# Chunked SSM scan plus SiLU MLP on one core: how unit 2 gets its decays, which queues carry the early loads, and the order of unit 0's scan

## The chip, the cores and the metric

The kernel runs on one core of one Trainium2 chip. The metric is device time in microseconds (us), median of three runs; lower is better. The core's engines each work through their own list of instructions in order: TensorE (PE, matrix products), VectorE (DVE), ScalarE (ACT), GpSimd (POOL), and SyncE (SP), which here only issues transfers. ACT and POOL can issue transfers too, from their own lists. An engine that waits for a semaphore holds everything behind it in its list.

## The reference

Two parts are computed, one feeding the other. First a state-space scan over x (batch 4, 8 heads, 768 steps, 32 values a step), with a decay a per step and vectors B and C of 16:

```python
log_a = np.log(np.clip(a, 1e-06, 1.0))
# per chunk: cum = cumsum(log_a); L = exp(cum_i - cum_j), causal
y = (C B^T * L) x + (C state) * exp(cum)
state = exp(sum(log_a)) * state + sum_j B_j x_j exp(cum_last - cum_j)
```

Then, with the heads of one step side by side (3072 rows of 256 values), a two-layer network: `h = x @ w_in` (256 to 2048), `g = h * sigmoid(h)`, `out = g @ w_out` (2048 to 256). The weights come in as float64.

## The kernel before, in words

**Units.** The 3072 rows are cut into 12 units of 256 steps, three per batch. A unit has four chunks of 64 steps (Q = 64). Units 0 to 2 are batch 0. The network works on pairs of units; P = 0 is the pair of units 0 and 1, which has its own start-up form, and P = 1 to 5 are the rest.

**One unit's scan.** The decays, bounded to [1e-6, 1], are needed in two layouts. `PZ[u]` (tiles pz, pz1, pz3: 4 chunks of 65, a row per head and state index) feeds the prefix products `PFX` (f_P, line 336). `ab[u]` (64 steps of a chunk broadcast over partitions, first column zero) feeds the decay matrices `E` (scan_E, line 344). f_T or f_TP make transposed B and C (bh, ct); f_T2 makes ce (line 391); f_C makes cw (line 395); f_B makes BT (line 368); f_G and f_D0 are the products C B and B x on PE (lines 425, 411); f_S and f_SM carry the state (lines 443, 445, 452); f_M multiplies by E (line 431); f_Y sums the unit's output on PE (465, 474), and f_X copies it to `XF[u]` (484). In the schedule texts the letters P, T, C, 1, 2, B, D, S, s, M, Y stand for these, so "2:PTC1" is a stretch of unit 2; "a" issues the next unit's ab, "L" all loads of a unit.

**Where the decays come from.** For units 0 and 1 raw a is loaded already broadcast (load_a, tile pa01) and bounded on chip (f_P0, line 332); their ab is made by PE from the tile ach with a selection matrix (f_Ab, line 351; f_A bounds ach, line 266). For units 2 to 11, all of a is loaded in chunk layout (tile acl, line 258), bounded (f_A2, line 272), and written to two arrays in DRAM, a_in and a_zero, by two transfers that ACT issues (273, 274). load_pa (106) and load_ab (113) read them back broadcast. The tiles ab and pz have one buffer each, so unit 3's ab may be loaded only when unit 2's E is done.

**Weights.** Sixteen blocks of 512 KB (load_w, 186), w0 to w7 of the first layer and w8 to w15 of the second, pass through six raw buffers. float64 becomes float32 by two ACT steps (w_size, lines 192 and 195: wu, wv), three DVE steps and an add on POOL (w_bits, 200 to 208: w32). Later each block is split into high, low and rest parts (w_h, w_l, w_d: steps h, l, d of the texts).

**The network.** For P = 0, f_s1(u, j) multiplies unit u with block j and applies SiLU (514, 517); f_s2 is the second layer (527; the steps m0 to m7). For the other pairs it is s1_d, s1_h, s1_g, s2 and s2_d (542, 550, 558, 560, 584, 585, 598), driven by step(s), with scans of later units in between. PSUM gives two buffers to f_s1's output, which f_TP's transposes and the dummy products of busy(n) share; TP's buffer is held until cw has read it.

**What sets the order.** The order on every engine is written out by hand (manual schedule): the calls at the top issue the first loads, a list of calls runs unit 0 and unit 1's scan, and the texts in `steps` and the loop behind it say what follows each f_s1 and f_s2: "b5" is w_bits(5), "s6" w_size(6), "r11" the load of block 11. Nearly all loads stand in SP's list. The program shares eight semaphores among the transfers that SP and ACT issue. An issue that takes a semaphore in turn waits until that semaphore's earlier transfer has landed, whichever of the two queues issued it. A tile with no free buffer makes the issue wait for the tile's last reader as well. Transfers issued by POOL have semaphores of their own.

Of the kernel before, what the change touches and what calls it, by code (L numbers as in the profile page):

```python
# [8 lines left out]
FP32 = mybir.dt.float32  # L9
# [24 lines left out]
def kernel(  # L34
# [69 lines left out]
    def load_pa(u, q):  # L104
        PZ[u] = pz if u != 3 else block("pz3")[:, 0:4 * Q + 4].rearrange("p (c t) -> p c t", c=4)
        q.dma_start(out=PZ[u].rearrange("p c t -> p (c t)"),
                    in_=a_in[:, 4 * u:4 * u + 4].rearrange("h (o c) t -> h o (c t)", o=1).to_broadcast([H, N, 4 * Q + 4]))

    def load_ab(u, q):
        ab[u] = loads.tile([128, 2, H, Q], FP32, name="ab")  # L110
        for t in range(4):
            k, c = divmod(t, 2)
            q.dma_start(out=ab[u][64 * c:64 * c + 64, k], in_=a_zero[4 * u + t:4 * u + t + 1].to_broadcast([64, H, Q]))
# [115 lines left out]
    a_in = dram.tile([H, batch * S // Q, Q + 1], FP32, name="a_in")  # L229
    a_zero = dram.tile([batch * S // Q, H, Q], FP32, name="a_zero")  # L230
    NC0 = S // Q
    A0, A1 = 96, 96 + NC0
    ach = block("ach").rearrange("p (h t) -> p h t", t=Q)
    nc.sync.dma_start(out=ach[A0:A1], in_=bass.AP(tensor=a.tensor, offset=a.offset, ap=[[Q, NC0], [S, H], [1, Q]]))
    pa01 = block("pa01")
# [4 lines left out]
    def load_a(u, q):  # L240
        q.dma_start(out=pa01[:, UT * u:UT * u + UT],
                    in_=bass.AP(tensor=a.tensor, offset=a.offset + UT * u, ap=[[S, H], [0, N], [1, UT]]))

    load_a(0, nc.scalar)
    load_t(0, 1, nc.sync)
    load_n(0, 0, nc.scalar)
    load_x(0, nc.sync)
    load_w(0, nc.sync)
    load_a(1, nc.sync)
    for n in range(1, 3):  # L250
        load_w(n, nc.sync)
    load_n(1, 0, nc.sync)
    load_n(1, 1, nc.sync)
    load_x(1, nc.sync)

    acl = block("acl").rearrange("p (h t) -> p h t", t=Q)
    for b in range(batch):
        nc.sync.dma_start(out=acl[NC0 * b:NC0 * b + NC0],
                          in_=bass.AP(tensor=a.tensor, offset=a.offset + b * H * S, ap=[[Q, NC0], [S, H], [1, Q]]))

    for n in range(3, RAW):
        load_w(n, nc.sync)
    load_n(2, 1, nc.sync)

    def f_A():
        nc.vector.tensor_scalar(out=ach[A0:A1], in0=ach[A0:A1], scalar1=1.0, scalar2=1e-6, op0=ALU.min, op1=ALU.max)
        nc.vector.memset(ach[A0:A1, :, 0:1], 0.0)

    def f_A2():

        r = slice(0, NC0 * batch)
        nc.vector.tensor_scalar(out=acl[r], in0=acl[r], scalar1=1.0, scalar2=1e-6, op0=ALU.min, op1=ALU.max)
        nc.scalar.dma_start(out=a_in[:, :, 1:].rearrange("h c t -> c h t"), in_=acl[r])
        nc.scalar.dma_start(out=a_zero[:, :, 1:], in_=acl[r, :, 1:])
# [5 lines left out]
    def f_A0():  # L280
        for t in (a_in[:, :, 0:1].rearrange("h c t -> c h t"), a_zero[:, :, 0:1]):
            nc.gpsimd.dma_start(out=t, in_=misc[:NC0 * batch, 0:H].rearrange("p (h t) -> p h t", t=1))
# [38 lines left out]
    nc.scalar.activation(diag, diag1.to_broadcast([128, H, Q]), AF.Copy)  # L321
# [330 lines left out]
    for e in range(2):  # L652
        f_T2(0, e)
# [243 lines left out]
```

## Time and profile before

| | |
|---|---|
| median of three runs | 341.19 us (339.53 to 342.89) |
| profiled execution | 342.16 us, of which the span 340.4 us |
| granted TensorE clock, mean | 0.988 of full |
| busy in the span | PE 322.7 us, DVE 251.7, ACT 219.0, POOL 71.4 |
| moved by the DMA engines | 30.85 MB, mean 91 GB/s |

The span runs from the first to the last instruction of the program; the rest of the time lies around it. The page's busy share of PE is an average over the whole span: where the profile is cut into windows, the start-up with P = 0 (about the first 63 us) looks unlike the rest. In the timeline, a bracket after a group of instructions gives the idle time of the engine just before it and what ended it. A name ending in q is an engine's sequencer, where transfers are issued. A float32 product shows as two records a call.

### The profile page before, as it was taken

The numbers are of one execution on the slowest core, as the hardware profiler recorded it, in microseconds if no ns is written. First come the engines' busy times: TensorE is split into PE (matmuls) and PEld (weight loads), VectorE is DVE, ScalarE is ACT, GpSimd is POOL, SyncE is SP. The second block draws the span as 40 slices with busy tenths as digits, with TensorE's granted clock in tenths as the row PEclk, the third lists the DMA queues.
The fourth block names the chain that finished last, engine by engine and source line by source line (L and its number), as shares of the span: only waits on it lengthen the run. The fifth ranks groups of instructions, "written<-read, shape, count | busy, mean of one in ns | idle before, by whom it ended". The sixth has DMA issues, their size and how long they took to land.

```text
span 340.4 us, 7774 instructions
## 1 busy us (share of the span) xinstructions
PE 322.7 (95%) x3136; PEld 256.8 (75%) x3136; DVE 251.7 (74%) x416; ACT 219.0 (64%) x418; POOL 71.4 (21%) x71
## 2 busy tenths in 40 slices
PE   7877994999999999999999999999999999999993
PEld 3556783888877778777778778778778778888882
DVE  6885784998568797998766897865996863484453
ACT  3645685376359889757775856676666756666651
POOL 4433240537101113033101331202231202000000
PEclk9997999899999999999999999999999999999999
DMA  6986869854665484244340153430153000012003
GB/s 144 192 217 167 251 143 325 199 97 77 122 135 88 92 159 79 58 112 79 64 95 0 43 113 66 91 67 0 48 109 64 2 2 0 0 24 40 0 0 62
DMA packets 97423, 30.85 MB, mean 91 GB/s; under 512 B 82284, under 2 KB 88684, under 8 KB 97388
## 3 DMA queue, kind: packets, MB, share of 16 engines
q1 hardware_dynamic: 87812, 25.32, 32.3%
q0 software_dynamic: 2368, 4.20, 7.0%
q10 hardware_dynamic: 7208, 0.85, 1.7%
q8 instruction: 24, 0.39, 0.5%
q14 instruction: 11, 0.09, 0.1%
HBM read 22.82 MB, written 3.34 MB: 77 GB/s over the span
## 4 chain that ended last, share of the span: by engine, by line
PE 83%; DMA 5%; SPq 5%; DVE 3%; ACT 1%; issue 1%; DVEq 0%; ACTq 0%
PE hp L550 23%; PE b L598 11%; PE hp L542 11%; PE oa L584 10%; PE oa L585 10%; PE oa L527 8%; PE hp L514 3%; SPq L123 2%; PE gy L474 2%; PE gy L465 2%; DMA tbc<-in_C_dram 2%; PE gy L425 2%; DMA ab<-a_zero 1%; DMA pz<-a_in 1%; DVE E L344 1%; SPq L186 1%
## 5 line engine op out<-in xcount | busy, mean ns | idle before, releaser
L544 ACT ACTIVATE hp<-hp 128x512 f32<-128x512 f32 x80 | 46.6, 582 | 74.6 <-PE hp L542 74.5
L564 DVE TENSOR_TENSOR gl<-g,gh 128x512 fp32r<-128x512 f32 x62 | 42.8, 690 | 53.0 <-ACT gh L560 49.8
L550 PE MATMUL hp<-xh,wh 128*128 128x512 f32 x160 | 65.4, 409 | 0.0
L568 DVE SCALAR_TENSOR_TENSOR gd<-gh,g 128x512 fp32r<-128x512 f32 x80 | 59.6, 748 | 5.2 <-ACT gh L560 5.2
L550 PE MATMUL hp<-xl,wl 128*128 128x512 f32 x160 | 62.7, 392 | 0.0
L584 PE MATMUL oa<-gh,wh 128*128 128x512 f32 x160 | 62.5, 391 | 0.0
L585 PE MATMUL oa<-gl,wl 128*128 128x512 f32 x160 | 62.5, 391 | 0.0
L564 POOL TENSOR_TENSOR gl<-g,gh 128x512 fp32r<-128x512 f32 x18 | 29.2, 1622 | 122.1 <-ACT gh L560 122.1
L560 ACT ACTIVATE gh<-g 128x512 fp32r<-128x512 f32 x80 | 50.5, 632 | 2.8
L542 PE MATMUL hp<-xd,wd 128*128 128x512 f32 x160 | 49.6, 391 | 0.0
L558 ACT ACTIVATE g<-hp 128x512 f32<-128x512 f32 x80 | 47.5, 593 | 0.5 <-PE hp L550 0.5
L598 PE MATMUL b<-gd,wd 128*128 128x512 f32 x160 | 44.4, 390 | 0.0
L550 PEld LDWEIGHTS hp<-xh,wh 128*128 128x128 f32 x160 | 30.0, 188 | 9.2 <-ACT hp L544 2.5
L514 PE MATMUL hp<-xf,w 128*128 128x256 f32 x128 | 32.8, 414 | 4.3 <-ACT xf L484 2.4
L542 PEld LDWEIGHTS hp<-xd,wd 128*128 128x128 f32 x160 | 30.0, 188 | 6.7
L598 PEld LDWEIGHTS b<-gd,wd 128*128 128x128 f32 x160 | 30.0, 188 | 6.6 <-DVE o L624 0.3
L584 PEld LDWEIGHTS oa<-gh,wh 128*128 128x128 f32 x160 | 30.0, 188 | 6.5
L585 PEld LDWEIGHTS oa<-gl,wl 128*128 128x128 f32 x160 | 30.0, 188 | 6.4
L550 PEld LDWEIGHTS hp<-xl,wl 128*128 128x128 f32 x160 | 30.1, 188 | 5.2
L514 PEld LDWEIGHTS hp<-xf,w 128*128 128x128 f32 x128 | 25.9, 207 | 9.8 <-POOL w L208 2.6
L344 DVE TENSOR_TENSOR_SCAN E<-ab,diag 128x512 f32<-128x512 f32 x24 | 28.4, 1209 | 4.8 <-DMA ab<-a_zero 4.7
L208 POOL TENSOR_TENSOR w<-wu,wv 128x512 uint32<-128x512 uint32 (+1 forms) x20 | 23.2, 1169 | 37.8 <-DVE wv L203 37.8
(84 smaller groups left out, 378.4 us busy)
## 6 DMA issues: line engine op xcount, KB each, us to landing
ab<-a_zero SPq DMA_DIRECT2D x40, 128.0 KB
raw<-in_moe_w_in_dram SPq DMA_DIRECT2D x8, 512.0 KB
raw<-in_moe_w_out_dram SPq DMA_DIRECT2D x8, 512.0 KB
wl<-w POOLq DMA_DIRECT2D x16, 256.0 KB, 3.2
xt<-in_x_dram SPq DMA_DIRECT2D x24, 128.0 KB
out_dram<-ot SPq DMA_DIRECT2D x44, 64.0 KB
tbc<-in_C_dram SPq DMA_DIRECT2D x22, 64.0 KB
pz<-a_in SPq DMA_DIRECT2D x10, 130.0 KB
```

The costliest lines, as they stand in the source:

```text
L344: nc.vector.tensor_tensor_scan(out=E[u].rearrange("p k h t -> p (k h t)")[:, Q * g0:Q * (g0 + n)], data0=t.rearrange("p g t -> p (g t)"), ...
L514: nc.tensor.matmul(out=hp[:, i], lhsT=two(w32[j])[:, kc, 128 * i:128 * i + 128], rhs=two(XF[u])[:, kc], start=(kc == 0), stop=(kc == KC - 1))
L542: nc.tensor.matmul(out=HP[s], lhsT=two(WD[f // 2])[:, kc, 128 * (f % 2):128 * (f % 2) + 128], rhs=XD[P][:, kc], start=(kc == 0), stop=Fals ...
L544: nc.scalar.activation(HP[s], HP[s], AF.Copy, scale=-HALF / UP)
L550: nc.tensor.matmul(out=HP[s], lhsT=two(w[f // 2])[:, kc, 128 * (f % 2):128 * (f % 2) + 128], rhs=x_[P][:, kc], start=False, stop=(kc == KC ...
L558: nc.scalar.activation(G[s], HP.pop(s), AF.Silu, scale=UP)
L560: nc.scalar.activation(GH[s], G[s], AF.Copy, scale=DOWN)
L564: engine.tensor_tensor(out=GL[s], in0=G[s], in1=GH[s].bitcast(FP32), op=ALU.subtract)
L568: nc.vector.scalar_tensor_tensor(out=GD[s], in0=GH[s].bitcast(FP32), scalar=1.0 + 1.0 / HALF, in1=G.pop(s), op0=ALU.mult, op1=ALU.subtract)
L584: nc.tensor.matmul(out=OA[P][m], lhsT=two(WH[n])[:, r, ms], rhs=gh, start=(f == 0), stop=False)
L585: nc.tensor.matmul(out=OA[P][m], lhsT=two(WL[n])[:, r, ms], rhs=gl, start=False, stop=(f == NF - 1))
L598: nc.tensor.matmul(out=B2[P][:, m], lhsT=two(WD[n])[:, r, 128 * m:128 * m + 128], rhs=gd, start=(fresh and s == tiles[0]), stop=True, skip ...
```

## The change

Unit 2 no longer takes its decays from a_in and a_zero. Raw a for it is loaded broadcast into a new tile pa2 and bounded by f_P0(2) on POOL. Its ab is read from a new DRAM array a_first, which SP writes from ach once f_A has bounded it. a_in, a_zero and acl hold batches 1 to 3 only (NC1 chunks), and their indices are shifted by NC0. Loading acl moves into a function f_A1, behind unit 1's scan; bounding it and storing a_in and a_zero (f_A2) comes later still, after w_bits(4), and SP issues the stores.

load_ab uses two transfers of 256 KB in place of four of 128 KB. Raw a for units 0 and 1 is one transfer on SP in place of two (one of them on ACT); unit 1's C moves to ACT's queue, near the front; unit 2's x is issued by POOL. Blocks w3 to w5 and unit 2's loads are issued inside f_A. Unit 3's C and B in transposed form, pz and bn are issued around block 10, its x after s1(1,2).

In unit 0, the E scans now come before C's transpose and the prefix products; f_P0 for units 0 and 1 runs on POOL; the tile diag is filled by DVE, not ACT; E, BT and B x are no longer done half by half; the dummy products are redistributed. w_size(0) is split, its first part ahead of sm(0). In the texts, unit 2's P, T, C and first E come one f_s1 earlier, w_bits of blocks 5 and 9 to 12 one or more steps later, unit 2's Y after s1(1,5), unit 3's products after s1(1,7), and unit 3's Y after m1.

```diff
@@ -104,13 +104,14 @@
     def load_pa(u, q):
         PZ[u] = pz if u != 3 else block("pz3")[:, 0:4 * Q + 4].rearrange("p (c t) -> p c t", c=4)
         q.dma_start(out=PZ[u].rearrange("p c t -> p (c t)"),
-                    in_=a_in[:, 4 * u:4 * u + 4].rearrange("h (o c) t -> h o (c t)", o=1).to_broadcast([H, N, 4 * Q + 4]))
+                    in_=a_in[:, 4 * u - NC0:4 * u - NC0 + 4].rearrange("h (o c) t -> h o (c t)", o=1).to_broadcast([H, N, 4 * Q + 4]))
 
     def load_ab(u, q):
         ab[u] = loads.tile([128, 2, H, Q], FP32, name="ab")
-        for t in range(4):
-            k, c = divmod(t, 2)
-            q.dma_start(out=ab[u][64 * c:64 * c + 64, k], in_=a_zero[4 * u + t:4 * u + t + 1].to_broadcast([64, H, Q]))
+        src, n = (a_first, 4 * u) if u < UPB else (a_zero, 4 * u - NC0)
+        for c in range(2):
+            q.dma_start(out=ab[u][64 * c:64 * c + 64].rearrange("p k h t -> p k (h t)"),
+                        in_=src[n + c:n + 4:2].rearrange("(o k) h t -> o k (h t)", o=1).to_broadcast([64, 2, H * Q]))
 
     def load_n(u, i, q):
         b, t0 = at(u)
@@ -226,52 +227,56 @@
                                        op0=ALU.mult, op1=ALU.subtract)
 
 
-    a_in = dram.tile([H, batch * S // Q, Q + 1], FP32, name="a_in")
-    a_zero = dram.tile([batch * S // Q, H, Q], FP32, name="a_zero")
     NC0 = S // Q
+    NC1 = NC0 * (batch - 1)
+    a_in = dram.tile([H, NC1, Q + 1], FP32, name="a_in")
+    a_zero = dram.tile([NC1, H, Q], FP32, name="a_zero")
+    a_first = dram.tile([NC0, H, Q], FP32, name="a_first")
     A0, A1 = 96, 96 + NC0
     ach = block("ach").rearrange("p (h t) -> p h t", t=Q)
     nc.sync.dma_start(out=ach[A0:A1], in_=bass.AP(tensor=a.tensor, offset=a.offset, ap=[[Q, NC0], [S, H], [1, Q]]))
-    pa01 = block("pa01")
+    pa01, pa2 = block("pa01"), block("pa2")
     pz1 = block("pz1")[:, 0:4 * Q + 4].rearrange("p (c t) -> p c t", c=4)
     pz = const.tile([128, 4, Q + 1], FP32, name="pz")
     one = const.tile([128, 4, Q + 1], FP32, name="one")
 
-    def load_a(u, q):
-        q.dma_start(out=pa01[:, UT * u:UT * u + UT],
-                    in_=bass.AP(tensor=a.tensor, offset=a.offset + UT * u, ap=[[S, H], [0, N], [1, UT]]))
-
-    load_a(0, nc.scalar)
+    def load_a(t, t0, n):
+        nc.sync.dma_start(out=t[:, 0:n], in_=bass.AP(tensor=a.tensor, offset=a.offset + t0, ap=[[S, H], [0, N], [1, n]]))
+
     load_t(0, 1, nc.sync)
     load_n(0, 0, nc.scalar)
+    load_n(1, 1, nc.scalar)
+    load_a(pa01, 0, 2 * UT)
     load_x(0, nc.sync)
-    load_w(0, nc.sync)
-    load_a(1, nc.sync)
-    for n in range(1, 3):
+    for n in range(3):
         load_w(n, nc.sync)
     load_n(1, 0, nc.sync)
-    load_n(1, 1, nc.sync)
     load_x(1, nc.sync)
-
-    acl = block("acl").rearrange("p (h t) -> p h t", t=Q)
-    for b in range(batch):
-        nc.sync.dma_start(out=acl[NC0 * b:NC0 * b + NC0],
-                          in_=bass.AP(tensor=a.tensor, offset=a.offset + b * H * S, ap=[[Q, NC0], [S, H], [1, Q]]))
-
-    for n in range(3, RAW):
-        load_w(n, nc.sync)
-    load_n(2, 1, nc.sync)
 
     def f_A():
         nc.vector.tensor_scalar(out=ach[A0:A1], in0=ach[A0:A1], scalar1=1.0, scalar2=1e-6, op0=ALU.min, op1=ALU.max)
         nc.vector.memset(ach[A0:A1, :, 0:1], 0.0)
+        nc.sync.dma_start(out=a_first, in_=ach[A0:A1])
+        load_w(3, nc.sync)
+        load_w(4, nc.sync)
+        load_a(pa2, 2 * UT, UT)
+        load_ab(2, nc.sync)
+        load_w(5, nc.sync)
+        load_n(2, 1, nc.sync)
+
+    acl = block("acl").rearrange("p (h t) -> p h t", t=Q)
+
+    def f_A1():
+        for b in range(1, batch):
+            nc.sync.dma_start(out=acl[NC0 * (b - 1):NC0 * b],
+                              in_=bass.AP(tensor=a.tensor, offset=a.offset + b * H * S, ap=[[Q, NC0], [S, H], [1, Q]]))
 
     def f_A2():
 
-        r = slice(0, NC0 * batch)
+        r = slice(0, NC1)
         nc.vector.tensor_scalar(out=acl[r], in0=acl[r], scalar1=1.0, scalar2=1e-6, op0=ALU.min, op1=ALU.max)
-        nc.scalar.dma_start(out=a_in[:, :, 1:].rearrange("h c t -> c h t"), in_=acl[r])
-        nc.scalar.dma_start(out=a_zero[:, :, 1:], in_=acl[r, :, 1:])
+        nc.sync.dma_start(out=a_in[:, :, 1:].rearrange("h c t -> c h t"), in_=acl[r])
+        nc.sync.dma_start(out=a_zero[:, :, 1:], in_=acl[r, :, 1:])
 
     misc = block("misc")
     idle = misc[:, 0:UT].bitcast(BF16)
@@ -279,7 +284,7 @@
 
     def f_A0():
         for t in (a_in[:, :, 0:1].rearrange("h c t -> c h t"), a_zero[:, :, 0:1]):
-            nc.gpsimd.dma_start(out=t, in_=misc[:NC0 * batch, 0:H].rearrange("p (h t) -> p h t", t=1))
+            nc.gpsimd.dma_start(out=t, in_=misc[:NC1, 0:H].rearrange("p (h t) -> p h t", t=1))
 
     def busy(n, small=0):
         t = half("zero")
@@ -318,7 +323,7 @@
     nc.gpsimd.affine_select(out=ident, in_=ident, pattern=[[-1, 128]], compare_op=ALU.not_equal,
                             fill=1.0, base=0, channel_multiplier=1)
     diag = const.tile([128, H, Q], FP32, name="diag")
-    nc.scalar.activation(diag, diag1.to_broadcast([128, H, Q]), AF.Copy)
+    nc.vector.tensor_copy(out=diag, in_=diag1.to_broadcast([128, H, Q]))
     par = const.tile([128, 2], FP32, name="par")
     for e in range(2):
         nc.vector.tensor_reduce(out=par[:, e:e + 1], in_=hm[:, e::2], op=ALU.add, axis=AX.X)
@@ -327,8 +332,8 @@
     E, BT, BH, CT, CE, CW, PFX, ST, SM, DP, GY, XF, BX = ({} for _ in range(13))
 
     def f_P0(u, engine):
-        src = pa01[:, UT * u:UT * u + UT].rearrange("p (c t) -> p c t", t=Q)
-        PZ[u] = (pz, pz1)[u]
+        src = (pa2[:, 0:UT] if u == 2 else pa01[:, UT * u:UT * u + UT]).rearrange("p (c t) -> p c t", t=Q)
+        PZ[u] = (pz, pz1, pz)[u]
         engine.tensor_scalar(out=PZ[u][:, :, 1:], in0=src, scalar1=1.0, scalar2=1e-6, op0=ALU.min, op1=ALU.max)
 
     def f_P(u):
@@ -646,31 +651,30 @@
                 in_=r[32 * q:32 * q + 32].rearrange("p (b d) -> p b d", d=32))
 
 
-    f_P0(0, nc.vector)
-    f_P(0)
+    f_P0(0, nc.gpsimd)
+    f_P0(1, nc.gpsimd)
+    f_Ab(0, 0)
+    f_Ab(0, 1)
+    f_TP(0)
+    busy(2, 18)
+    f_Ek(0, 0)
+    f_Ek(0, 1)
+    f_B(0)
+    f_D0(0)
     f_T(0, 1)
     for e in range(2):
         f_T2(0, e)
+    w_size(0, "u")
+    f_P(0)
     f_C(0, nc.gpsimd)
-    f_P0(1, nc.gpsimd)
     f_A0()
-    f_Ab(0, 0)
-    f_Ab(0, 1)
-    f_TP(0)
-    busy(0, 18)
+    busy(1, 10)
     f_G(0)
-    f_Ek(0, 0)
-    f_B(0, slice(0, 1))
-    f_D0(0, (0, 1))
-    busy(1, 10)
-    f_Ek(0, 1)
-    f_B(0, slice(1, 2))
-    f_D0(0, (2, 3))
     f_S(0)
     f_SM(0)
+    w_size(0, "v")
     f_M(0, 0)
     f_M(0, 1)
-    w_size(0)
     w_bits(0, 2)
     f_Ab(1, 0)
     w_size(1)
@@ -691,6 +695,7 @@
     load_n(2, 0, nc.scalar)
     f_P(1)
     f_C(1)
+    f_P0(2, nc.gpsimd)
     w_bits(2, 2)
     f_G(1)
     f_D0(1)
@@ -700,21 +705,19 @@
     f_M(1, 0)
     f_M(1, 1)
     f_s1(0, 2)
-    f_A2()
     load_w(6, nc.sync)
-    load_pa(2, nc.sync)
-    load_ab(2, nc.sync)
+    load_x(2, nc.gpsimd)
+    f_A1()
     load_w(7, nc.sync)
-    load_x(2, nc.sync)
     load_w(8, nc.sync)
     w_bits(3, 2)
-    w_size(4, "u")
     f_Y(1)
     f_X(1)
-    w_size(4, "v")
+    w_size(4)
     w_bits(4)
+    f_A2()
+    load_bcx(3, "c")
     load_w(10, nc.sync)
-    load_bcx(3, "cx")
     load_pa(3, nc.sync)
     load_bcx(3, "b")
     w_size(5)
@@ -725,6 +728,8 @@
                 load_unit(u)
             elif c == "a":
                 load_ab(u + 1, nc.sync)
+            elif c == "x":
+                load_x(u, nc.sync)
             elif c == "T":
                 if 0 < u < UPB:
                     f_TP(u)
@@ -774,13 +779,13 @@
             n = int(step[1:].split(".")[0])
             {"b": w_bits, "s": w_size, "h": w_h, "l": w_l, "d": w_d, "m": f_s2, "p": s1_d, "r": load_r}[step[0]](n)
 
-    steps = ((1, 0, ""), (0, 3, "b5 r11 s6"), (1, 1, "2:PTC1"), (1, 2, "b6 r12 s7 2:2Ba"), (1, 3, "b7 r13 s8"),
-             (0, 4, "2:DSsM"), (1, 4, "b8 r14 s9"), (0, 5, "2:Y b9 r15 s10"), (1, 5, "3:TPC"), (0, 6, "3:12B s11"),
-             (1, 6, "b10 s12 h0 l0"), (0, 7, "3:DSsM 2:h"), (1, 7, "b11 s13"))
+    steps = ((1, 0, ""), (0, 3, "2:PTC1 s6"), (1, 1, "b5 2:2Ba"), (1, 2, "3:x b6 r11 s7"), (1, 3, "b7 r12 s8"),
+             (0, 4, "2:DSsM r13"), (1, 4, "b8 r14 s9"), (0, 5, "s10"), (1, 5, "2:Y 3:TPC"), (0, 6, "3:12B s11"),
+             (1, 6, "b9 r15 s12 h0 l0"), (0, 7, "2:h"), (1, 7, "3:DSsM b10 s13"))
     for u, j, text in steps:
         f_s1(u, j)
         todo(text)
-    for text in ("m0 b12 2:l 3:Y 4:L h1 l1 2:d d0 s14", "m1 3:h h2 l2 d1 b13 s15", "m2 3:l 3:d d2 b14 h3 l3",
+    for text in ("m0 b11 2:l h1 l1 d0 s14", "m1 3:Y b12 2:d 4:L 3:h h2 l2 d1 b13 s15", "m2 3:l 3:d d2 b14 h3 l3",
                  "m3 b15 p0 d3 h4 l4 4:T", "m4 h8 l8 d4 h5 l5 d8", "m5 d5 h9 l9 d9"):
         todo(text)
 
```

## The prediction

> **What bounds the kernel now.** I read the table of windows first, cut where TensorE (PE) changes its state. Columns: window, its length, busy time (and instructions) of PE, weight loads, VectorE (DVE), ScalarE (ACT), GpSimd (POOL), then granted clock, DMA share, GB/s.
>
> ```profile
> 0.00:27.26 27.26, 20.50 (x396) 13.03 (x397) 20.90 (x49) 13.56 (x29) 11.19 (x25) 1.00 0.83 183
> 27.26:30.70 3.44, 3.44 (x11) 2.92 (x12) 3.14 (x6) 2.53 (x5) 1.38 (x1) 0.70 0.70 180
> 30.70:54.76 24.06, 23.42 (x274) 19.08 (x273) 15.62 (x27) 15.72 (x31) 7.30 (x5) 0.97 0.75 212
> 54.76:59.24 4.48, 0.00 (x1) 0.00 (x1) 2.82 (x4) 2.86 (x6) 0.00 (x0) 1.00 0.98 312
> 59.24:63.26 4.02, 4.02 (x41) 3.26 (x42) 3.84 (x11) 1.16 (x3) 2.16 (x2) 0.58 0.75 226
> 63.26:340.40 277.14, 271.31 (x2416) 218.55 (x2415) 205.39 (x323) 183.12 (x346) 49.40 (x38) 1.00 0.33 64
> ```
>
> From 63.26 us PE is busy 271.3 of 277.1 us at full clock. Only its matmuls bound that part, and the change leaves it the same matmuls. So I need one number: when the second product's first step (m0, L527) starts. Before, that is 63.09 us. PE's timeline shows what delays it; brackets hold idle time and its releaser.
>
> ```profile
> 21.48 1.99 PE L514 MATMUL hp<-xf,w 128*128 128x256 f32 x8 [1.33 <-POOL w L208]
> ...
> 27.26 7.13 PE L514 MATMUL hp<-xf,w 128*128 128x256 f32 x24 [2.37 <-ACT xf L484]
> ...
> 59.24 0.65 PE L411 MATMUL gy<-xt,BT 64*32 64x64 f32 x32 [4.48 <-DVE BT L368]
> 59.82 3.44 PE L514 MATMUL hp<-xf,w 128*128 128x256 f32 x8
> ```
>
> The last row is the second cost of a stall: 8 records in 3.44 us, while the 8 at 21.48 took 1.99. Finer windows show the clock at 0.50 from 29 to 32 us and from 60 to 62 us. The chain of waits says what is behind the two long gaps (start, length, what).
>
> ```profile
> 20.94 5.31 DMA tbc<-in_C_dram
> 26.27 0.66 ACT wu L192
> 26.93 0.28 ACT xf L484
> 27.26 5.42 PE hp L514 x16
> ...
> 51.40 4.87 DMA ab<-a_zero
> ...
> 59.24 0.65 PE gy L411 x32
> ```
>
> ACT stood 2.16 us (24.1 to 26.3): f_A2 had put two stores on ACT's queue (L273 at 23.60, L274 at 25.55), and the second waited for a semaphore of a load still in flight. Unit 1's xf, behind it, came late. The large gap is unit 3's ab: SP issued it only at 50.84, behind x, pz, bn and two weight blocks, and DVE waited 4.65 us for it.
>
> **What the Trainium skill says.** "DMA: Bandwidth & Descriptors", section "Issuing engines are not separate DMA queues": all issuing engines share the same 16 DMA engines, so a second queue saves only issue time. The trace agrees: from 22 to 30 us q1 took 71.3% and q10 26.6% of the same engines. I therefore give three queues no bandwidth. "TensorE: Matmul & The Clock Gate", section "Part 1: The HAM clock gate": after an idle window of about 3.4 us the clock is halved, and about 3.4 us of work restores it. The trace agrees on the cost (0.50 for some 3.4 us, so 1.7 us lost), but 2.37 us of idle time was enough.
>
> **Start, 0 to 20 us.** E(0) no longer stands behind the transpose at 5.67, but PE's first ab product ends near 4.7, so DVE gains up to 0.9. Against it: diag moves to DVE (0.61 on ACT; no DVE row of it exists, I take 0.4 to 0.6 from L200's 0.42 and ACT's time; hidden, since DVE waits for ab then); both P0 go to POOL (0.40 each), and a's first load (now 256 KB) stands behind C's four on SP, with C(1) on ACT beside it, 128 KB sooner. Block 0 then comes about 1 us later, its add too. I take 0, with both ends 0.7. Dummy matmuls are moved and two added; they sit in gaps.
>
> **pa2 is the new wait.** P0(2) stands on POOL ahead of block 2's add, and both halves of bn(2) on ACT, ahead of sm(1), wait for the semaphores of w4 and pa2. Ahead of pa2's landing stand, in KB: ach 24, C(0) 128, pa01 256, bn(0) 128, C(1) 128, x(0) 256, w0 to w4 2560, bn(1) 128, x(1) 256, a_first 24, pa2 128: 4016 KB, 4.11 MB. At the 183 GB/s of the first window that is 22.5 us; at 83% share it could be some 20.5 were the engines always fed. I take 22.0. Then P0(2) 0.40 and half an add 0.7: s1(0,2) starts at 23.1, not 21.48. PE is then idle 2.9 us, so the slow clock (1.7) comes here. ACT issues bn(2) by 22.7 and sm(1) (0.69) is done by 23.4, hidden by s1(0,2). Then 1.9 + 1.7 for s1(0,2), 1.5 for Y(1), 0.4 for xf, which no store delays: s1(1,0) at 28.6 at full clock. Before: 27.26 plus 1.7 of slow clock still to come, 28.96. Net -0.4; with pa2 at 20.5, no slow clock and s1(1,0) at 25.9, -3.
>
> **Unit 2.** pfx(2) waited 1.99 us for pz; now it stands on DVE behind the bounding of batches 1 to 3 (L272's step), which waits for acl. Bytes to acl: 4.11 + ab 0.52 + w5 0.52 + bn 0.13 + C 0.13 + x 0.26 + w6 0.52 + acl 0.07 = 6.27 MB. At 183 GB/s 34.3 us, at 212 (third window) 29.6; I take 32. Plus 0.41, 0.70 and 0.42 (L272, L336, L395): cw at 33.6, and s1(1,2), which needs the buffer that cw reads, at about 34.0 to 34.6 (PE itself, from 28.6 over three steps of 1.87 and TP 0.4, is there at 34.6; from 25.9, at 31.9, it would wait). Before, 35.08. I take 34.1: unit 2's G at 34.1 + 5.45 = 39.5 (before 40.46). E(2) and BT(2) on DVE take 1.2 + 1.5 + 1.2 + 0.6 more, to 38.1, so BT's gap of 0.39 goes. x(2) goes through POOL: two issues, each between 0.9 (L221) and 2.4 (L282's 0.89 for 384 pieces, scaled to 1024). It holds block 3's add until at most 28.5 + 1.4; s1(0,3) needs that near 30.
>
> **Unit 3.** ab(3) now stands on SP after w10, pz and bn and ahead of w11, w12 and x(3); it needs E(2), done near 37.5. Before, issue to use was 5.5 us with two blocks ahead; so at most 43.5. PE needs it after G and D (1.0), three s1 (5.5), Y(2) (1.4) and s1(0,6): 49.3. Six us of slack: the 4.48 and its slow clock of 1.7 go. What is late next is DVE itself: from cw(2) to BT(3) it has some 17 us of work, 20 with the stretches the trace shows (1.38 instead of 0.43), done by 51 to 54; D(3), now behind s1(1,7), comes at 54.7. From G(2): 1.0 + 7 x 1.83 + 1.4 + 1.0 gives m0 at 55.7, 7.4 earlier than 63.09.
>
> **Second product.** b10 moves behind unit 3's M on DVE, so the chain to xd(3) is some 13 to 14.8 us after m0; the first s1_d needs it at 15.1 (before, 5.5 us of slack). I charge 0.5. Weights have ended their loads by then: w10 is issued near 35. Loads of ab in two issues of 256 KB, not four of 128: same bytes, and that stretch waits for none of them. Sum: 342.16 - 7.4 + 0.5 = 335.3 for the profiled execution (span 340.40 and 1.76 around it). It lies 0.97 over the median 341.19, so 334.3 there; I say 334.5.
>
> **Rivals.** (A) The wait is only moved: acl or its neighbours land at 35 or 36, DVE stands before pfx(2), cw comes at 37, PE waits 3 us and slows by 1.7. For it: DVE has nothing else in that stretch, and DMA share is already 0.75 to 0.98. Against: w6 is the only block between C(2) and acl. It leaves 1.5 to 4 us of gain, 337 to 340. (B) Slower. One late pa2 holds POOL, ACT and through them PE, since w2's add, sm(1), Y(1) and xf(1) are in line behind it. The point is where the delay eats 6.9 us: landing at 29. At 32 it gives 345. For it: pa2 queues behind w3 and w4 and shares engines with bn(2). Against: it needs 4.11 MB at 142 GB/s or less, where 183 were seen. (C) The change doesn't do what it says: unit 3 stays late because ab(3)'s buffer or SP's order holds it as before. Then only the first 1.3 us remain, 340. Against: two blocks and x(3) are no longer ahead of it.
>
> **How the numbers follow.** Forecast 0.68 (331.8 to 337), A 0.14, C 0.06, B 0.12, of which half lies over 344.6. One per cent, about what a measurement of this kernel can tell from no change, is 3.4 us: faster is under 337.8, slower over 344.6. Forecast and a fifth of A: 0.71 faster; 0.06 slower, raised to 0.09 for a start that costs more than I see; 0.20 same. The range runs from 331.8 (pa2 at 20.5) to 340.5 (A and C).
>
> **What would show it.** Right: no wait of E for ab before unit 3's D; no clock of 0.5 near 60 us; m0 at 54 to 57 us; ACT without an idle stretch between s1(0,2) and xf(1). The new waits: POOL on pa2 near 22 us, ACT's bn issue likewise, DVE on acl near 32. Wrong: PE idle over 3 us between 20 and 35, an m0 after 60, or gaps after m0 that before doesn't have.

## The result and the profile after

| | before | after |
|---|---|---|
| median | 341.19 us (338.39 to 342.89, 13 runs) | 337.09 us (335.23 to 338.46, 13 runs) |
| ratio, 95% interval | 1 | 0.9887 (0.9859 to 0.9916) |
| profiled execution, span | 342.16, 340.4 | 338.14, 336.4 |
| mean clock granted to TensorE | 0.988 | 0.986 |
| busy: PE, DVE, ACT, POOL | 322.7, 251.7, 219.0, 71.4 | 322.9, 251.9, 218.1, 75.7 |

The changed kernel is faster by 4.1 us. The forecast was 6.7 us (341.19 to 334.5), so it has the sign and is inside its range, but the gain is six tenths of what was predicted. In the two profiled executions the gain is 4.0 us, where the sum had 6.9. The question for the runs is where the other 2.9 us are.

The table of windows of the kernel after is cut at the end of unit 1's B x (21.16), then at the start of s1(0,2), of s1(1,0), of unit 2's C B product, of the second product (m0) and of the first s1_d. Columns: window, length, then busy time and instructions of PE, weight loads, DVE, ACT and POOL, the granted clock, DMA share and GB/s.

```profile
0.00:21.16 21.16, 18.22 (x294) 10.70 (x294) 16.25 (x37) 9.93 (x20) 9.32 (x22) 1.00 0.83 193
21.16:23.74 2.58, 0.01 (x2) 0.00 (x0) 2.47 (x7) 0.87 (x3) 1.18 (x3) 0.87 0.96 274
23.74:30.18 6.44, 5.96 (x105) 4.42 (x105) 2.14 (x4) 1.99 (x5) 3.85 (x5) 0.52 1.20 236
30.18:41.69 11.51, 11.26 (x53) 9.45 (x53) 8.41 (x14) 9.62 (x19) 4.05 (x2) 1.00 0.75 231
41.69:58.33 16.64, 16.15 (x274) 13.11 (x273) 12.71 (x23) 11.54 (x24) 6.16 (x5) 1.00 0.79 224
58.33:74.85 16.52, 15.57 (x163) 13.13 (x153) 15.78 (x25) 9.34 (x19) 7.89 (x6) 1.00 0.64 121
```

The same cuts in the kernel before, for the last two of them:

```profile
40.46:63.09 22.63, 17.76 (x273) 14.46 (x273) 16.71 (x32) 14.06 (x28) 6.83 (x6) 0.92 0.83 245
63.09:78.21 15.12, 15.12 (x153) 13.05 (x152) 14.95 (x22) 8.32 (x16) 7.70 (x7) 1.00 0.61 117
```

The stretch from unit 2's C B product to m0 shrank from 22.63 to 16.64 us: these 6.0 us are more than the whole gain of 4.0, and other stretches gave some back. The stretch behind it grew from 15.12 to 16.52 us, although PE has the same work in it. And one stretch, 23.74 to 30.18, ran at a clock of 0.52.

PE's timeline after shows what stands at these cuts (start, length, group; in brackets the idle time before and its releaser).

```profile
15.47 1.89 PE L519 MATMUL hp<-xf,w 128*128 128x256 f32 x8
...
23.74 3.78 PE L519 MATMUL hp<-xf,w 128*128 128x256 f32 x8 [2.57 <-POOL w L209]
...
30.18 3.72 PE L519 MATMUL hp<-xf,w 128*128 128x256 f32 x16 [0.47 <-ACT xf L489]
...
57.94 0.45 PE L416 MATMUL gy<-xt,BT 64*32 64x64 f32 x32
58.33 7.17 PE L532 MATMUL oa<-gT,w 128*128 128x256 f32 x32
...
74.85 0.73 PE L547 MATMUL hp<-xd,wd 128*128 128x512 f32 x2 [0.94 <-DVE xd L509]
```

Unit 3's B x (57.94), which waited 4.48 us before, follows without a gap. VectorE's timeline, before and then after, shows why: E of unit 3 no longer waits for ab.

```profile
56.39 2.34 DVE L344 TENSOR_TENSOR_SCAN E<-ab,diag 128x512 f32<-128x512 f32 x2 [4.65 <-DMA ab<-a_zero]
```

```profile
50.52 2.33 DVE L349 TENSOR_TENSOR_SCAN E<-ab,diag 128x512 f32<-128x512 f32 x2
```

The new waits are the one ahead of s1(0,2), whose 8 records took 3.78 us, and the one ahead of the first s1_d. The chain of waits and POOL's timeline name the source of the first:

```profile
17.50 4.81 DMA pa<-in_a_dram
...
22.48 0.09 POOL pz L337
...
22.95 0.74 POOL w L209
```

```profile
22.48 0.39 POOL L337 TENSOR_SCALAR pz<-pa 128x256 f32<-128x256 f32 x1 [3.68 <-DMA pa<-in_a_dram]
22.95 1.42 POOL L209 TENSOR_TENSOR w<-wu,wv 128x256 uint32<-128x256 uint32 x2
```

pa2 landed at 22.31 us (17.50 + 4.81). POOL had been idle 3.68 us for it, with the add of weight block 2 behind it.

### The profile page after: what moved, and what is told of

It reads as the page before. It is cut to its first block, busy times and chain, and to the rows that moved or that the text cites. A ratio compares the mean times of both kernels' runs of the same rounds, so it can differ in the third digit from the quotient of the medians.

```text
span 336.4 us, 7749 instructions
## 1 busy us (share of the span) xinstructions
PE 322.9 (96%) x3138; PEld 256.4 (76%) x3138; DVE 251.9 (75%) x415; ACT 218.1 (65%) x417; POOL 75.7 (23%) x75
## 4 chain that ended last, share of the span: by engine, by line
PE 79%; DVE 10%; DMA 5%; issue 2%; SPq 1%; ACT 1%; POOL 0%; DVEq 0%; ACTq 0%; POOLq 0%
PE hp L555 23%; PE hp L547 11%; PE b L603 11%; PE oa L589 11%; PE oa L590 11%; PE oa L532 4%; PE gy L479 2%; PE hp L519 2%; DMA tbc<-in_C_dram 2%; PE gy L470 2%; PE gy L430 2%; DVE wv L204 2%; DVE E L349 2%; DMA pa<-in_a_dram 1%; DMA xt<-in_x_dram 1%
## 5 line engine op out<-in xcount | busy, mean ns | idle before, releaser
L547 PEld LDWEIGHTS hp<-xd,wd 128*128 128x128 f32 x160 | 29.9, 188 | 7.8 <-DVE xd L509 1.3
L519 PE MATMUL hp<-xf,w 128*128 128x256 f32 x128 | 31.4, 401 | 4.2 <-POOL w L209 2.9
L519 PEld LDWEIGHTS hp<-xf,w 128*128 128x128 f32 x128 | 24.8, 199 | 9.4 <-POOL w L209 3.9
L209 POOL TENSOR_TENSOR w<-wu,wv 128x512 uint32<-128x512 uint32 (+1 forms) x20 | 24.0, 1207 | 33.4 <-DVE wv L204 33.3
```

Source lines behind the costliest of these rows:

```text
L519: nc.tensor.matmul(out=hp[:, i], lhsT=two(w32[j])[:, kc, 128 * i:128 * i + 128], rhs=two(XF[u])[:, kc], start=(kc == 0), stop=(kc == KC - 1))
L547: nc.tensor.matmul(out=HP[s], lhsT=two(WD[f // 2])[:, kc, 128 * (f % 2):128 * (f % 2) + 128], rhs=XD[P][:, kc], start=(kc == 0), stop=Fals ...
```

## The steps of the sum against the trace

Each row is the difference after minus before, cut as above. "Forecast" is worked out from the times in the prediction (for example s1(1,0) to unit 2's C B product: 39.5 − 28.6 = 10.9, before 13.20, so −2.3).

| stretch | forecast | first profile of after | forecast missed by |
|---|---|---|---|
| start to first s1 | 0 | +1.0 (15.47, before 14.45) | +1.0 |
| to s1(0,2) | +1.6 | +1.2 | −0.4 |
| to s1(1,0) | −0.3 | +0.7 | +1.0 |
| to unit 2's C B product | −2.3 | −1.7 | +0.6 |
| to m0 | −6.4 | −6.0 | +0.4 |
| to the first s1_d | +0.5 | +1.4 | +0.9 |
| rest | 0 | −0.6 | −0.6 |
| sum | −6.9 | −4.0 | +2.9 |

Three terms of about 1 us each were off: the start, the stretch at half clock, and VectorE behind m0. The experiments take them one by one. Ratios in them are to the kernel before, run on the same chip beside each.

## Experiments

**The changed kernel again**, unedited, for what one execution differs from another.

> The changed kernel, unedited, profiled a second time. Theory (the half clock after the 2.57 us gap is drawn anew in every execution, in steps of 3.4 us): the starts of all work up to s1(0,2) agree with the first profile within some 0.3 us, but the stretch at 0.50 that lasted from 23 to 30 us has another length, none or 3.4 us, and the time moves by half of the difference, 1.7 or 3.4 us. Rival (the stretch belongs to the schedule): 6.8 us of half clock again.

336.08 us median (335.48 to 336.93, 6 runs), ratio 0.9864 (0.9816 to 0.9911); profiled execution 336.08. The clock in the windows is 1.00 from the start to the first s1_d. PE's timeline and one window:

```profile
23.13 1.99 PE L519 MATMUL hp<-xf,w 128*128 128x256 f32 x8 [1.59 <-POOL w L209]
...
27.01 3.72 PE L519 MATMUL hp<-xf,w 128*128 128x256 f32 x16 [0.47 <-ACT xf L489]
```

```profile
23.13:27.01 3.88, 3.41 (x104) 2.69 (x104) 2.86 (x6) 2.74 (x7) 2.48 (x4) 1.00 1.30 221
```

Here the gap ahead of s1(0,2) is 1.59 us, not 2.57, and from s1(0,2) to s1(1,0) it takes 3.88 us, not 6.44. The starts agree with the first profile only to 0.4 us at the first s1 (15.85) and 0.6 us at s1(0,2), not to the 0.3 expected, and the gap itself differs: this pair does not show that one and the same gap goes both ways. m0 starts at 56.20 (forecast 55.7) and unit 2's C B product at 39.29 (forecast 39.5). PE waits 0.81 us for unit 2's B (bn, at 31.65), a wait that the prediction has no term for. DVE's timeline of this execution also shows the wait for acl that the prediction put at 32:

```profile
31.90 0.42 DVE L277 TENSOR_SCALAR acl<-acl 36x512 f32<-36x512 f32 x1 [2.15 <-DMA acl<-in_a_dram]
```

**A warm TensorE ahead of s1(0,2).** Dummy products, which change no output, fill the gap.

```diff
     f_M(1, 1)
+    busy(10)
     f_s1(0, 2)
```

> The changed kernel with ten dummy products more on TensorE ahead of s1(0,2), in the gap in which it waits for block 2's add. Every wait stays as it was. Theory (the gap costs more by the clock than by its length): s1(0,2) still starts near 23.7, the clock is 1.00 all through 20 to 60 us, s1(0,2) lasts 1.99 and not 3.78, m0 starts near 55.7, the runs lie closer together than the 3.2 us of the changed kernel, and the median falls by 0.8 to 1.7 us. Rival (the loads decide what comes after, by acl): m0 stays near 58 at full clock.

336.03 us median (335.31 to 336.94, 6 runs), ratio 0.986 (0.9817 to 0.9904). s1(0,2) starts at 23.14 and takes 1.99 us, s1(1,0) starts at 27.02, the clock is 1.00. These are the times of the repeat above, to 0.01 us. So the step from s1(0,2) to s1(1,0) of the first profile lost 2.6 us to the half clock and to nothing else. The median is no lower than that of the repeat (336.08), because the repeat had hardly any half clock to lose.

**The kernel before again**, unedited.

> The kernel before, unedited, profiled a second time. Theory (the stretches at half clock are drawn anew in every execution, before as after): starts of work agree with the first profile up to 27 us, but the two stretches of 3.4 us at 0.50 (28.6 to 32.0 and 59.4 to 62.8) are not both there, m0 starts 1.5 to 3.4 us earlier than 63.1, and the whole time is below 342.16 by as much. Rival (gaps of 2.4 and 4.5 us always halve the clock): both stretches again, m0 near 63, 341.5 or more.

341.90 us median (339.83 to 342.92, 20 runs), ratio 1.0022 (0.9999 to 1.0045). PE's timeline and one window of it:

```profile
57.40 0.68 PE L411 MATMUL gy<-xt,BT 64*32 64x64 f32 x32 [5.54 <-DVE BT L368]
58.01 3.78 PE L514 MATMUL hp<-xf,w 128*128 128x256 f32 x8
```

```profile
56.90:63.70 6.80, 6.30 (x45) 4.98 (x46) 6.57 (x15) 2.88 (x6) 3.35 (x3) 0.50 0.87 214
```

Unit 3's wait is there again (5.54 us, 4.48 in the first profile), now with 6.8 us of half clock behind it; in turn, xf(1) waited only 0.82 us (2.37 in the first), with no half clock. So the half clock moved, but its sum of 6.8 us did not change: m0 starts 1.5 us earlier (61.58), and the execution is only 0.3 us shorter, less than expected. Single stalls differ between executions; the wait for unit 3's ab stays. The mean clock of whole runs says how much half clock each kernel had: its median is 0.985 over these 20 runs of before and 0.993 over the 13 of after (0.986 over all 95 runs of before on record and 0.994 over the 19 of after), and the profiles without half clock in the start-up have 0.996 to 0.999. As an estimate from these, with 0.997 for no half clock, before lost (0.997 − 0.985) × 340 = 4.1 us and after (0.997 − 0.993) × 336 = 1.3 us.

**The order of unit 0's scan undone.** T and the C B product come ahead of the E scans again.

```diff
     f_P0(1, nc.gpsimd)
+    f_T(0, 1)
+    for e in range(2):
+        f_T2(0, e)
     f_Ab(0, 0)
...
     busy(2, 18)
+    f_G(0)
     f_Ek(0, 0)
...
     f_D0(0)
-    f_T(0, 1)
-    for e in range(2):
-        f_T2(0, e)
...
     busy(1, 10)
-    f_G(0)
     f_S(0)
```

> The changed kernel with the old order inside unit 0 only: C's transpose and ce ahead of the E scans, and C B ahead of B x on TensorE. Theory (pa2 is the wait that decides): st comes after BT and B x alone, the first s1 starts near 14.5 us and not 15.5, s1(0,1) near 17.2, but s1(0,2) still starts near 23.7, since pa2 lands near 22.3 as before; the 1.0 us is waited away and the median is within 0.5 us of the changed kernel's 337.1. Rival (the scan order itself costs): everything comes 1.0 us earlier, 336.1.

337.12 us median (336.61 to 338.58, 6 runs), ratio 0.9893 (0.9862 to 0.9924). The first s1 starts at 14.38 us (15.47 after; before 14.45), so the order of the scan is what costs 1.0 us at the start. In the trace of after, the state starts only when unit 0's C B product on PE (9.89 to 10.59) is done, whose inputs stand behind the E scans on DVE; before, that product ran at 7.58. The state reads only B x, which was done at 9.19, but the program writes both products into one tile (new_dp). The median did not move, but not for the reason given: s1(0,2) did not stay at 23.7.

```profile
22.45 3.19 PE L519 MATMUL hp<-xf,w 128*128 128x256 f32 x8 [2.37 <-POOL w L209]
```

pa2 came earlier as well (POOL bounded it at 21.20, not 22.48), yet the gap of 2.37 us was long enough to halve the clock, and five of the six runs had a mean clock of 0.992 to 0.994. The 1.0 us of the start was eaten one step later.

**Weight block 2 ahead of pa2 on POOL.**

```diff
     f_C(1)
-    f_P0(2, nc.gpsimd)
     w_bits(2, 2)
+    f_P0(2, nc.gpsimd)
```

> The changed kernel with the bounding of pa2 moved behind block 2's add on GpSimd. Theory: the add no longer waits for pa2, s1(0,2) starts near 22.4 and not 23.7, TensorE's gap before it shrinks from 2.57 to about 1.3 us and the clock stays at 1.00 from 23 to 30 us, so s1(1,0) starts near 26.5 and not 30.2. Then cw of unit 2 decides, which stands behind acl (landed near 31.8): s1(1,2) near 34 and not 36.6, and the median falls by 2 to 3 us, to 334 to 335. Rival (loads bound the start whatever stands in line): some other load ends the wait, under 1 us.

336.19 us median (336.00 to 336.51, 6 runs), ratio 0.9862 (0.9834 to 0.9890): 0.9 us under the 337.09 of after, less than expected, and not told apart from the repeat of after. The gap ahead of s1(0,2) is 1.33 us, there is no half clock in the start-up, and the six runs lie within 0.5 us of each other. PE's timeline shows where the rest went:

```profile
22.20 1.99 PE L519 MATMUL hp<-xf,w 128*128 128x256 f32 x8 [1.33 <-POOL w L209]
...
33.34 5.45 PE L519 MATMUL hp<-xf,w 128*128 128x256 f32 x24 [0.85 <-DVE cw L400]
...
72.31 0.74 PE L547 MATMUL hp<-xd,wd 128*128 128x512 f32 x2 [1.12 <-DVE xd L509]
```

s1(1,0) comes at 26.08, but s1(1,2) then waits for cw, which stands behind acl: DVE idles 3.31 us for acl and bounds it at 31.70. The two late loads of unit 2 are in series: time won at the first is waited away at the second.

**Both edits together.**

> Both edits: old order inside unit 0, and the bounding of pa2 behind block 2's add. Theory: s1(0,2) near 21.4, full clock, and then the same wait for acl as with the second edit alone, so 0 to 0.7 us better than it: 333.5 to 335. Rival (no wait for acl): the two edits add, 3.5 us or more off 337.1.

336.56 us median (335.78 to 338.10, 6 runs), ratio 0.9885 (0.9851 to 0.9919). The first s1 starts at 14.29, s1(1,0) at 25.52, but unit 2's transposes wait for bn and s1(1,2) for cw:

```profile
30.61 0.33 PE L386 MATMUL tp<-ident,bn 128*128 128x128 f32 x1 [1.27 <-DMA bn<-in_B_dram]
33.09 5.45 PE L519 MATMUL hp<-xf,w 128*128 128x256 f32 x24 [0.19 <-DVE cw L400]
```

m0 is at 55.38, against 55.62 with the edit on POOL alone. So what the start costs is real, but most of it is hidden here: PE cannot pass unit 2's loads anyway.

**VectorE's order behind unit 3.** The edit on POOL, and two vector moves: block 7's bits behind unit 2's products, block 10's ahead of unit 3's.

```diff
-    ... (1, 3, "b7 r12 s8"), (0, 4, "2:DSsM r13"), ... (1, 7, "3:DSsM b10 s13")
+    ... (1, 3, "r12 s8"), (0, 4, "2:DSsM b7 r13"), ... (1, 7, "b10 3:DSsM s13")
```

> The kernel with block 2's add ahead of pa2's bounding (336.2), and two moves on VectorE: block 7's bits behind unit 2's st and M, and block 10's ahead of unit 3's st. Theory (VectorE's order makes the new gap at the first s1_d, and TensorE's short wait for gT near 44 us): the 1.1 us wait for xd goes, the 0.8 us wait for gT too, the stretch from m0 to the first s1_d is 15.2 and not 16.7 us, the median falls by 1.5 to 2 us. Rival (xd is late by ScalarE or by its loads): m0 to s1_d stays at 16.7, under 0.5 us.

334.05 us median (332.97 to 334.63, 6 runs), ratio 0.9798 (0.9755 to 0.9841): 2.1 us under the edit on POOL alone. DVE's timeline of after, and then of this kernel:

```profile
58.69 0.23 DVE L448 COPY st<-gy 128x64 f32<-128x64 f32 x1 [3.98 <-PE gy L416]
...
73.04 1.75 DVE L509 SCALAR_TENSOR_TENSOR xd<-xh,xf 128x512 fp32r<-128x512 f32 x1
```

```profile
55.48 0.22 DVE L448 COPY st<-gy 128x64 f32<-128x64 f32 x1 [1.10 <-PE gy L416]
...
67.47 1.86 DVE L509 SCALAR_TENSOR_TENSOR xd<-xh,xf 128x512 fp32r<-128x512 f32 x1
```

In after, DVE idles 3.98 us for unit 3's products with block 10 in line behind them. xd's second half then ends at 74.79, 16.5 us after m0. With block 10 in that idle time it ends 14.1 us after m0 (55.21). These 2.3 us are about block 10's three steps (60.98 to 62.45 in after) and one stretched instruction less. The stretch from m0 to the first s1_d is 15.23 us with PE never idle, against 16.69 with the edit on POOL alone. In these two profiles another 0.4 us lies before m0 and 0.3 behind the first s1_d. The two moves were not run apart. The stretch:

```profile
55.21:70.44 15.23, 15.23 (x162) 13.16 (x153) 14.58 (x24) 9.15 (x19) 8.06 (x7) 1.00 0.76 137
```

**Unit 3's ab earlier, in the kernel before.** One cause alone: two weight loads (blocks 11 and 12) no longer stand ahead of ab(3) on SP. In the first, ACT keeps the two stores; in the second SP takes them.

```diff
-    ... (0, 3, "b5 r11 s6"), ... (1, 2, "b6 r12 s7 2:2Ba"), (1, 3, "b7 r13 s8"),
+    ... (0, 3, "b5 s6"), ... (1, 2, "b6 s7 2:2Ba r11"), (1, 3, "b7 r12 r13 s8"),
```

> The kernel before, with one part of the change in kind: unit 3's ab loads are issued ahead of blocks 11, 12 and 13, not behind 11 and 12. Theory (unit 3's wait is the one that carries the gain): the wait of E for ab shrinks from 4.65 us to 1 to 2, TensorE's gap of 4.48 to under 2, and the clock near 60 us stays up; m0 starts at 58 to 59.5 us and not 63.1, the median falls by 3.5 to 4.5 us. Rival (transfers are short of bandwidth, so the two blocks then become late in its place): ScalarE waits for blocks 11 and 12 and the gain is under 1 us.

339.39 us median (337.33 to 342.15, 14 runs), ratio 0.9961 (0.9932 to 0.9990). PE's timeline:

```profile
28.29 7.13 PE L514 MATMUL hp<-xf,w 128*128 128x256 f32 x24 [3.65 <-ACT xf L484]
...
56.15 0.46 PE L411 MATMUL gy<-xt,BT 64*32 64x64 f32 x32 [0.35 <-DVE BT L368]
57.80 1.99 PE L514 MATMUL hp<-xf,w 128*128 128x256 f32 x8 [1.20 <-ACT gT L517]
```

The 4.48 us became 0.35 and 1.20, and m0 moved from 63.09 to 59.63. The median moved by 1.5 us only, less than expected: in this profile xf(1) waits 3.65 us, with half clock behind it, and the median clock of the 14 runs, 0.985, is no higher than that of before. SP's order thus is one cause of unit 3's wait, and its removal alone is worth about a third of the change.

> The kernel before with two parts: unit 3's ab ahead of blocks 11 to 13 (339.4 alone), and the stores of a_in and a_zero issued by SP, not by ScalarE. Theory (ScalarE's wait at its store makes the first long gap): the 2 us in which ScalarE stands behind the store go, TensorE's gap before s1(1,0) falls from 2.4 to 3.7 us to about 0.5, the clock near 28 to 32 us stays up, and the median falls by 1 to 2 us against 339.4. Then unit 2's pz decides, so not more. Rival (unit 2's own loads are what pays): no change against 339.4.

338.93 us median (335.49 to 342.36, 13 runs), ratio 0.9928 (0.9895 to 0.9960). The edit is the one above and, in f_A2, `nc.sync.dma_start` for the two `nc.scalar.dma_start`. PE's timeline:

```profile
25.47 5.45 PE L514 MATMUL hp<-xf,w 128*128 128x256 f32 x24 [0.55 <-ACT xf L484]
...
33.37 5.45 PE L514 MATMUL hp<-xf,w 128*128 128x256 f32 x24 [2.02 <-ACT gT L517]
...
55.68 0.46 PE L411 MATMUL gy<-xt,BT 64*32 64x64 f32 x32 [1.99 <-DVE BT L368]
57.01 3.38 PE L514 MATMUL hp<-xf,w 128*128 128x256 f32 x8 [0.87 <-ACT gT L517]
```

Without stores on ACT, xf(1) is in time. But 2.02, 1.99 and 0.87 us are waited away later, and m0 is at 60.23. By the ratios this kernel and the one ahead of it are not told apart, and two small edits do not do what the change does. What makes the rest was not isolated: neither unit 2's way to its decays nor load_ab's two transfers in place of four had a run of its own.

**All edits, and unit 2's loads earlier.** The start's old order, block 2 first on POOL, the vector moves; unit 2's B on SP instead of ACT, with C ahead of ab(2) and block 5; acl ahead of block 6.

```diff
         load_a(pa2, 2 * UT, UT)
+        load_n(2, 0, nc.sync)
+        load_n(2, 1, nc.sync)
         load_ab(2, nc.sync)
         load_w(5, nc.sync)
-        load_n(2, 1, nc.sync)
...
-    load_n(2, 0, nc.scalar)
...
-    load_w(6, nc.sync)
     load_x(2, nc.gpsimd)
     f_A1()
+    load_w(6, nc.sync)
```

> All edits together on the changed kernel: old order inside unit 0, block 2's add ahead of pa2's bounding, the two moves on VectorE, and of the loads: unit 2's bn issued by SP with its C ahead of ab and w5, and acl ahead of w6. Theory (each of the short waits left is a load that stands behind weight blocks): TP of unit 2 no longer waits for bn, s1(0,2) starts near 21.4, s1(1,0) near 25.2, m0 at 53 to 54 us against 55.2, the median falls to 332 to 333. Rival (block 5 or 6 takes their place on ScalarE): m0 near 55, 334.

336.52 us median (333.87 to 339.18, 6 runs), ratio 0.9847 (0.9789 to 0.9906). ACT's timeline:

```profile
30.68 0.66 ACT L193 ACTIVATE wu<-raw 128x512 f32<-128x512 f32 x1 [4.20 <-DMA raw<-in_moe_w_in_dram]
```

The rival holds: block 5 is late instead, ACT stands 4.20 us for it, and PE, which needs ACT for gT, 3.59 us, with half clock behind that; m0 is at 57.58. The same bytes pass; only their order changed.

**The same, with the work that block 5 feeds moved too.** acl stands ahead of blocks 5 and 6, and block 5's steps follow s1(1,1), one place later in the texts.

```diff
         load_a(pa2, 2 * UT, UT)
-        load_ab(2, nc.sync)
-        load_w(5, nc.sync)
+        load_n(2, 0, nc.sync)
         load_n(2, 1, nc.sync)
+        load_ab(2, nc.sync)
...
-    load_w(6, nc.sync)
     load_x(2, nc.gpsimd)
     f_A1()
+    load_w(5, nc.sync)
+    load_w(6, nc.sync)
...
-    w_size(5)
...
-    ... (0, 3, "2:PTC1 s6"), (1, 1, "b5 2:2Ba"), (1, 2, "3:x b6 r11 s7"), ...
+    ... (0, 3, "2:PTC1"), (1, 1, "s5 b5 2:2Ba"), (1, 2, "s6 3:x b6 r11"), (1, 3, "s7 r12"), ...
```

> The changed kernel with the old order of unit 0's scan, the second part of unit 2's load behind a weight block, the two vector moves of the units 2 and 3 before other work, and, new here: unit 2's B loaded on SP's queue ahead of unit 3's a, and unit 2's second state load issued ahead of weight blocks 5 and 6 with block 5's steps kept one turn later. Theory: unit 2's projection then finds its B (no wait near 28.8 us), the bounded state comes two or three microseconds earlier than its 32.4, unit 2's first score product starts near 31.5 us instead of 33.1, the main products near 53 and the first s1_d near 68.5; median 332, against 334.05 with the vector moves alone. Rival: weight blocks 5 and 6 come late in turn and hold ScalarE or VectorE as in the kernel with all edits; then the wait only changes its name, the main products stay near 55 and the median is 334 or more.

333.00 us median (331.49 to 333.82, 8 runs), ratio 0.9806 (0.9782 to 0.9830). PE's timeline:

```profile
29.62 7.17 PE L519 MATMUL hp<-xf,w 128*128 128x256 f32 x32 [0.25 <-ACT gT L522]
...
52.95 7.17 PE L532 MATMUL oa<-gT,w 128*128 128x256 f32 x32
```

The expectation calls acl the "bounded state" or "second state load" and s1(1,2) the "score product". No wait for bn or cw is left, and acl is bounded at 27.70; s1(1,2) starts at 31.45, m0 at 52.95 and the first s1_d at 68.18, all within 0.4 us of what the theory put down. The profiled execution, 331.49, is the fastest of the eight, and the median is 1.0 us above the 332 expected. By the ratios this kernel and the one with the vector moves alone (0.9798) are not told apart. Both intervals lie below that of after (0.9859 to 0.9916); that of the repeat (0.9816 to 0.9911) they overlap, though all six runs with the vector moves, taken on the same chip as the repeat's six, are faster than any of these.

## Why the prediction was right in sign and too large

**Right, with its number.** Unit 3's wait for ab is gone, in both profiles of after, and with it the slow clock near 60 us. m0 was put at 55.7; it came at 56.20 in one profile and at 58.33 in the other. pa2 was put at 22.0 and landed at 22.31, with POOL's block 2 behind it as told; acl was put at 32, and in the repeat DVE waited for it until 31.90 (in the first profile DVE came to it only at 32.39, without a wait). ACT's issue of bn(2) was to be over by 22.7 and was at 22.76, and xf(1) waited for nothing but PE. None of the rivals came: DVE's wait for acl (2.15 us in the repeat) stayed off PE's path there, pa2 was 6.7 us ahead of the point from which B decides, and ab(3) was in time. The landing of pa2 was derived from bytes; the chain of waits shows that it was issued only at 17.50, as SP's issue of unit 1's x took until 15.9, so the agreement is in part luck. This was read in the trace, not tested.

**Mis-sized: the slow clock.** The step "PE is then idle 2.9 us, so the slow clock (1.7) comes here" took one stretch of 3.4 us at half clock. The first profile has twice that, 23.1 to 29.9, the repeat none. The time from s1(0,2) to s1(1,0) was 6.44 and 3.88 us, and the run with a warm TensorE shows that the difference is the clock alone. That is 2.6 us where 1.7 was charged: nearly all of the +1.0 of that row. In the profiled pair the clock gave next to no gain, since before lost half of 3.4 + 3.4 and after half of 6.8. Over all runs it gave some 2.8 us, by the estimate from the mean clocks. A sum made from one execution cannot carry such a term: in the two profiles of after it was 2.6 us and nothing, and the last section shows on what that hangs.

**Mis-sized: VectorE behind m0.** "The chain to xd(3) is some 13 to 14.8 us after m0", 0.5 charged. It took 16.5 us and cost 1.4. Four vector instructions on this chain are stretched, each by 0.9 to 1.1 us (xd 1.75 against 0.69 for its first half). Without these 4.2 us it would have ended 12.3 us after m0, so the upper end of 14.8 left room for two of them. POOL's timeline of after shows an add of a weight block beside each of the four; the last two are these:

```profile
68.80 1.77 POOL L209 TENSOR_TENSOR w<-wu,wv 128x512 uint32<-128x512 uint32 x1 [0.96 <-DVE wv L204]
...
72.61 1.63 POOL L209 TENSOR_TENSOR w<-wu,wv 128x512 uint32<-128x512 uint32 x1 [1.07 <-DVE wv L204]
```

They end at 70.57 and 74.24, and the vector instructions that began meanwhile (69.35 and 73.04) end 0.55 us after each. The Trainium skill, page "SBUF — State Buffer", section "SBUF: two separate sides", says that VectorE, in an instruction with two inputs in SBUF or in a two-port mode, and GpSimd take a shared pair of ports as an exclusive lock, held for a whole instruction. The trace agrees; no run took the adds away. So each block's bits that move into a stretch bring their own three instructions and one such stall. The moved step, block 10, is the cause that the trace points to: with it back ahead of unit 3's products the stretch fell from 16.69 to 15.23 us. The 2.1 us by which the median fell are those of both vector moves.

**Mis-sized: the start.** "I take 0, with both ends 0.7" was +1.0. The step priced the scans and loads, but not that unit 0's state comes after its C B product, whose inputs now stand behind the scans. Its weight in the end is less than its size: undone alone or with the edit on POOL it moved m0 by little, as unit 2's loads hold PE in the same place.

**Two more rows.** The +0.6 up to unit 2's C B product is a slip in the sum: the prediction has PE itself at s1(1,2) at 34.6 when s1(1,0) starts at 28.6, but goes on from 34.1. From 34.6 the stretch is 11.45 us; it took 11.51. The +0.4 up to m0 is a wait that the sum left out: PE stands 0.49 us for gT at 46.88 (0.76 in the repeat), since ACT first waits for unit 2's state behind weight bits on DVE. With block 7's bits moved behind unit 2's products this wait was gone (one of 0.60 us for gT came later, at 52.27).

**The lower end.** The landing of pa2 at 20.5 does not follow from its own figures (22.5 × 0.83 is 18.7), and with pa2 there s1(1,0) would come at 25.4 by the same steps, not 25.9. Neither enters the forecast itself, only the lower end of its range.

**Open.** The −0.6 behind the first s1_d is no larger than kernels with the same work there differ (261.55 to 262.13 us among the profiles of after and its edits up to the vector moves).

## What to carry to other kernels

When a wait is removed, list the next late thing on every engine, since waits in series return only the last one's worth: here pa2, bn and acl, then block 5, each took its turn. A step that waits should have ready work ahead of it, not behind it: block 10 placed behind unit 3's products cost about 1.5 us, although VectorE had stood idle for 3.98 us just ahead of it. Price a gap on TensorE by its length and by what the clock may lose after it, and take that second part from several executions.

## What the runs showed of the hardware that was not expected

Whether a gap is followed by half clock is not decided by its length. In the kernel before with unit 3's ab earlier and the stores on SP, a gap of 2.02 us (before 33.37) had no half clock behind it, and one of 1.99 us (before 55.68) had 3.4 us of it. Within one execution the clock changes only at moments that lie whole steps of 3.41 us apart, counted from its first full step; in before, the two stretches start at 28.64 and 59.36, nine steps apart. Cut at these steps, the two gaps look different (the columns are those of the table after; the clock is the third number from the end):

```profile
29.13:32.54 3.41, 2.22 (x13) 1.73 (x11) 0.81 (x2) 1.51 (x3) 1.27 (x1) 1.00 0.60 194
32.54:35.96 3.42, 2.59 (x12) 2.31 (x13) 2.31 (x4) 2.34 (x6) 0.00 (x0) 1.00 0.72 221
...
53.02:56.44 3.42, 1.13 (x65) 0.73 (x64) 2.73 (x6) 1.20 (x3) 0.00 (x0) 1.00 0.92 316
56.44:59.85 3.41, 2.84 (x7) 2.30 (x8) 3.27 (x9) 3.07 (x7) 1.28 (x1) 0.50 1.04 396
```

The first gap is split between two steps (1.2 and 0.8 us idle); the second lies in one, which has 2.3 us idle with the short gaps around it. The same holds in all 13 traces: from full clock, a step with 1.90 us or more of idle TensorE was followed by half clock each time (21 steps, 13 of them at the end of the program), and one with up to 1.88 us never (the ends of matmuls are modelled, so the border is only as exact as that). In the first profile of after, the step from 19.66 to 23.07 has just 1.90 us idle; in the repeat, the step with the gap has 1.59. So whether a gap of two to three us is paid for twice depends, by this count, on where the steps happen to lie. A stretch lasts one step or two; what ends it these runs do not settle (a step at half clock with 0.57 us idle was the last, one with 0.54 was not).

The Trainium skill, page "TensorE: Matmul & The Clock Gate", section "Part 1: The HAM clock gate", gives an idle window of about 3.4 us and as much to recover, and says that the window runs free of the kernel, so that cold stretches vary from run to run. The free-running window and the variation agree; that 1.90 us idle within one window sufficed, and that stretches of 6.8 us occur, does not, and the measurement decides. As each stretch of 3.4 us costs up to 1.7 us, the spread of the runs goes with it: the six runs of the edit on POOL, with mean clocks of 0.994 to 0.998, lie within 0.5 us, while the 13 of after, with 0.986 to 0.999, lie within 3.2 us.
